# A fused attention and MoE kernel: a new opening list and a new end list, with batch 3's projection further back

## The chip, the cores and the metric

The kernel runs on one core of one Trainium2 chip. Times are device microseconds (us) of one execution; lower is better. The engines are TensorE (PE in the profile; PEld is its weight load), VectorE (DVE), ScalarE (ACT), GpSimd (POOL) and SyncE (SP). Each works through its own instructions in program order and waits on semaphores for the others. Transfers are asked for by POOL (loads from memory that change float32 to bfloat16) or by SP (stores, small reshaping copies, transposes).

## The reference, cut to what matters

```python
def _attn_ref(q, k, v, E, F):                 # q, k, v: 8 batches x 8 heads x 1024 x 64
    k_proj = np.einsum('ks,bhsd->bhkd', E, k)  # the sequence of 1024 projected to 64
    v_proj = np.einsum('ks,bhsd->bhkd', F, v)
    scores = scale * np.matmul(q, k_proj.transpose(0, 1, 3, 2))
    attn = np.exp(scores - np.max(scores, axis=-1, keepdims=True))
    attn = attn / (np.sum(attn, axis=-1, keepdims=True) + 1e-09)
    return np.matmul(attn, v_proj)

def _moe_ref(x, w_in, w_out):                 # x: 8192 x 512, w_in: 512 x 2048, w_out: 2048 x 512
    h = x @ w_in
    g = h * (1.0 / (1.0 + np.exp(-1.702 * h)))
    return g @ w_out
```

The output of the attention, with the heads side by side, is the x of the second function.

## The kernel before, in words

The 8192 tokens are cut into 16 blocks of 512; block j belongs to batch b = j // 2. For a batch, k and v (two loads, line 58, asked for by POOL) are projected with E and F on TensorE (step `pj`, line 671), the projected k is copied (`kb`) and transposed by a DMA of SP (`kd`), the projected v is copied (`vq`). The queries of the batch are loaded in eight pieces (line 70) and transposed by one DMA of SP (`qd`, line 239). For a block there are then scores (`sc`), exponentials on ACT (`ex`), sums (`su`, `den`), the reciprocal of the sums, which takes a way through small DMAs (`ga`, `rc`, `sr`, `sb`), the product with v (`va`), and the division (`mv`). After that come the two large products of the second function. Both are made with seven instead of eight block products (a Strassen form): steps `u0.P1` to `u3.P7` for the first (line 607, four matmuls each), `F1.0` to `F7.1` for the second (line 504, eight matmuls each), with sums of inputs (`xs`, `gs`) and of results (`c1` to `c3`, `d1`, `d2`, `Fc`, `Fd`, `Fo`) on DVE and ACT, and the gelu on ACT (`g11` to `g22`). `st0` and `st1` store half a block of output each.

No scheduler decides an order when the kernel is built. After a prologue, the order is written out by hand in three lists: OPEN, then STEPS, which is repeated for j = 4 to 12, then TAIL. A word such as `pj@6:0` or `kb@6/A` is a step for block 6, with its PSUM bank after the colon and its engine (A for ACT, D for DVE) after the slash. Each step's instructions go to the queues of their engines in the order of the list; there, only the order among steps of one engine and the waits for data remain. A step of SP or POOL that stands late in the list can therefore start early, when nothing holds it.

Two steps ask for loads, and both begin with a tiny copy on POOL into a tile `held`, which makes POOL wait for a chosen event:

```python
        elif i == "ld":
            nc.gpsimd.tensor_copy(held[:, 1], qT[b][:1, J - 1, 0, :1])
            load_kv(k, kt, b + 1, "k_sb")
            load_kv(v, vt, b + 1, "v_sb")
```

So `ld` of batch b waits until that batch's queries are transposed (line 674), and only then asks for k and v of batch b + 1. There is one buffer for k and one for v, so the load also waits for `pj` of batch b. `lq` (line 693) does the same for the queries, waiting for the broadcast `rbc` of the block before. For this case the steps `ld@4` (asks for k and v of batch 3), `pj@6` (projects batch 3), `qd@4` and `qd@6` (transpose the queries of batches 2 and 3) matter most.

Of the kernel before, what the change touches and what calls it, by code (L numbers as in the profile page):

```python
# [17 lines left out]
def kernel(ctx, tc, q, k, v, E, F,  # L18
                                                     moe_w_in, moe_w_out, out):
    nc = tc.nc  # L20
    B, H, S, D = q.shape
# [255 lines left out]
    xs = {}  # L277
# [98 lines left out]
    def ffn2_ops(j):  # L376
# [8 lines left out]
        qda@2 sc.0@1:7,6 sc.1@1:5,4 ex.0.1@1 O.3.0@0:0 ex.1.1@1 ex.1.0@1 ex.0.0@1 O.2.0@0:2 O.1.0@0:1 O.3.1@0  # L385
        tk.2.1@1:6 tk.0.1@1:3 tk.1.1@1:4 tk.0.0@1:5 tk.2.0@1:7 gt@4 O.2.1@0 O.3.2@0 tr.0.0@1 tr.0.1@1 tm.0.1@1
        tm.0.0@1 O.2.2@0 tr.1.1@1 xt.0@1:3 tm.1.1@1 tk.1.0@1:4 O.3.3@0 O.1.1@0 O.2.3@0 tr.2.1@1 tr.1.0@1
        tm.1.0@1 tm.2.1@1 tr.2.0@1 oc.3@0/A tm.2.0@1 O.1.2@0 xt.2@1:6 xt.1@1:0 tk.3.0@1:5 tk.3.1@1:4 xc.2@1/A
        ws.1@1 tr.3.1@1 O.0.0@0:7 O.0.1@0 tr.3.0@1 O.0.2@0 tm.3.1@1 xc.0@1/A tm.3.0@1 xt.3@1:3 O.0.3@0 xc.3@1/A
        xc.1@1/D L.11@1:5 O.1.3@0 L.1@1:4 ws.2@1 ws.0@1 Lg.11@1 oc.2@0/A Lg.1@1 wi.5@1/A oc.0@0/D ws.3@1  # L390
        L.13@1:6 L.3@1:3 L.0@1:7 ws.4@1 pj@2:4 Lg.13@1 vq.0@2/D vx.0@2 Lg.0@1 L.8@1:6 Lg.3@1 kb@2/A oc.1@0/D
        L.14@1:0 L.2@1:2 L.5@1:5 Lg.8@1 kd@2 L.12@1:1 L.4@1:3 Lg.5@1 Lg.14@1 qdb@2 L.6@1:7 L.7@1:0 Lg.12@1
        Lg.4@1 s0.1@0 Lg.6@1 L.10@1:1 L.9@1:3 ws.5@1/D vx.1@2 Lg.7@1 vq.1@2/A Lg.10@1 Lg.2@1 L.15@1:5 Lg.9@1
        Lg.15@1 wi.4@1 sc.1@2:4,6 sc.0@2:7,0 F1.0@1:2 F1.1@1 ex.0.0@2 ex.1.1@2 gs1.0@1 sc.1@3:5,3 ex.1.1@3
        sc.0@3:7,6 Fc1@1:1/D lq@2 gs1.1@1 ex.0.1@3 F2.0@1 ex.1.0@3 ex.0.0@3 s0.0@0 F2.1@1 su@3:7,5 ex.0.1@2
        tk.0.0@2:6 gs3.1@1 gs2.1@1 gs2.0@1 den.0@3/A F6.0@1 den.1@3/D tr.0.0@2 ex.1.0@2 tk.1.0@2:7 tk.1.1@2:0
        tk.0.1@2:3 tm.0.0@2 gs4.1@1 tr.0.1@2 tr.1.0@2 tm.0.1@2 tm.1.0@2 tr.1.1@2 F5.0@1:6 F6.1@1 tk.2.0@2:7
        tk.2.1@2:4 tm.1.1@2 gs3.0@1 F5.1@1 xt.0@2:3 Fc2@1/A xt.1@2:0 tr.2.1@2 tr.2.0@2 ga@3 Fc3@1/A tm.2.0@2
        xc.0@2/A F7.1@1 Fo0@1/A gt@6 tm.2.1@2 xc.1@2/A tk.3.0@2:4 gs4.0@1 xt.2@2:7 tk.3.1@2:3 tr.3.0@2 tr.3.1@2
        rc@3 F3.0@1 xc.2@2/D tm.3.0@2 F3.1@1 F7.0@1 sr@3 u0.P1@2:0 tm.3.1@2 xs.0@2 u1.P5@2:3 u1.P1@2:4 Fd1@1  # L400
        xt.3@2:7 F4.0@1 u0.c1@2:5/D Fd2@1 xc.3@2/A u1.c1@2:2/D u1.c3@2/A xs.1@2 F4.1@1 u0.P2@2 u1.P6@2 xs.3@2
        u1.P3@2 u0.P6@2 u1.P2@2 u2.P1@2:6 Fo1@1/D u1.c2@2/D xs.2@2 u1.P7@2 u0.P5@2:1 u0.c2@2/A u0.g11@2 u1.d2@2
        gt@7 ld@2 u0.P7@2 qd@4 u1.d1@2 u0.c3@2/D u0.d1@2 u1.g11@2 u1.P4@2 u3.P1@2:0 u1.g21@2 u0.P3@2 pj@4:4
        u2.P5@2:2 u1.g22@2 u1.g12@2 u0.d2@2 u0.g12@2 u2.c1@2:3/A kb@4/A u3.c1@2:1/D u2.P6@2 u2.c2@2/D u3.P6@2
        u0.g22@2 u2.P2@2 u3.P5@2:7 u2.c3@2/D vq.1@4/A vq.0@4/D u2.P7@2 u0.P4@2 u3.P2@2 ld@4 u3.c3@2/D u3.c2@2/A
        u3.P7@2 u2.g11@2 u3.g11@2 u3.P3@2 u2.P3@2 u2.d1@2 sb@3 u2.g22@2 u0.g21@2 kd@4 gs1.0@2 u2.P4@2 u3.d1@2
        u2.d2@2 va.0@3:4,5 u2.g21@2 gs2.0@2 u3.P4@2 F1.0@2:3 u3.d2@2 F1.1@2 mv.0.1@3 st0@1 mv.0.0@3 va.1@3:5,7
        u3.g22@2 u2.g12@2 u3.g21@2 u3.g12@2 sc.0@4:4,6 gs1.1@2 Fc1@2:1/A sc.1@4:0,2 F2.0@2 F2.1@2 ex.1.0@4
        ex.1.1@4 ex.0.1@4 xs.0@3 ex.0.0@4 mv.1.1@3 gs2.1@2 F6.0@2 gs4.0@2 Fo0@2/A F6.1@2 st1@1 gs3.0@2
        sc.1@5:6,2 ex.1.1@5 mv.1.0@3 sc.0@5:0,7 su@4:3,4 u0.P1@3:5 xs.1@3 Fc2@2/D den.1@4/A ex.0.1@5 den.0@4/D  # L410
        F5.0@2:2 ex.1.0@5 xs.2@3 u1.P5@3:3 u0.P5@3:7 u0.c1@3:6/D u1.P1@3:4 gs3.1@2 u0.c3@3/D ex.0.0@5 gs4.1@2
        u0.P2@3 u0.g11@3 pj@6:0 xs.3@3 ga@4 u1.c1@3:5/A kb@6/A u0.P3@3 u0.P6@3 u0.c2@3/D u0.d2@3 F7.1@2 F5.1@2
        vq.0@6/A vq.1@6/A u1.P2@3 rc@4 u1.c3@3/A u1.g11@3 su@5:0,7 u0.P7@3 F7.0@2 u0.d1@3 den.1@5/D u1.P6@3
        u1.P3@3 u0.P4@3 u1.c2@3/A u3.P1@3:7 Fc3@2/D den.0@5/A gt@1 lq@4 u0.g12@3 u2.P1@3:4 Fd1@2 F4.0@2
        u3.c1@3:0/D u3.P6@3 u3.P2@3 u1.d2@3 u1.P7@3 kd@6 F4.1@2 u1.g12@3 u2.c1@3:3/D u0.g21@3 u3.g11@3 u0.g22@3
        u1.d1@3 u1.g22@3 sr@4 u2.P6@3 u2.P5@3:6 u3.c2@3/A u1.P4@3 u2.P2@3 u3.P5@3:7 u2.c2@3/A Fo1@2/D u2.g11@3
        u2.c3@3/D u2.P3@3 u2.d2@3 qd@6 u1.g21@3 F3.1@2 sc.1@6:6,4 u3.c3@3/D sc.0@6:5,1 u2.P7@3 F3.0@2 u2.d1@3
        gs1.0@3 ex.1.1@6 u3.P3@3 u2.P4@3 u3.P7@3 sb@4 ga@5 Fd2@2 u3.d1@3 ex.0.1@6 F1.0@3:4 st0@2 gs2.0@3 u3.d2@3
        ex.0.0@6 ex.1.0@6 F1.1@3 u3.P4@3 Fc1@3:1/D va.0@4:6,7 mv.0.1@4 u2.g21@3 va.1@4:5,3 u3.g21@3 F2.1@3
        F2.0@3 mv.0.0@4 st1@2 mv.1.0@4 u2.g22@3 u2.g12@3 u3.g12@3 xs.0@4 u0.P1@4:7 mv.1.1@4 u3.g22@3 u1.P1@4:0  # L420
        u0.c1@4:5/A u1.P5@4:6 gs1.1@3 xs.1@4 Fo0@3/A gs2.1@3 u0.P2@4 gs4.1@3 u1.c1@4:2/A gs3.0@3 xs.3@4 u0.g11@4
        F5.0@3:3 xs.2@4 u1.P2@4 rc@5 u1.c3@4/A gt@5 F6.0@3 F6.1@3 u0.P5@4:7 u1.P6@4 u0.P6@4 u1.P3@4 Fc2@3/D
        F5.1@3 u1.c2@4/D u0.c3@4/A sr@5 u0.c2@4/A u0.P3@4 u1.g11@4 gt@2 u3.P1@4:4 gs3.1@3 u0.P7@4 F7.1@3 F7.0@3
        u0.d2@4 u1.d2@4 u0.d1@4 gs4.0@3 u0.P4@4 Fc3@3/A Fd1@3 gt@3 u1.P7@4 su@6:6,7 F4.0@3 den.1@6/A u3.P5@4:7
        u1.d1@4 u3.c1@4:0/A u3.P2@4 u0.g21@4 den.0@6/A F4.1@3 Fo1@3/D u1.g12@4 u2.P1@4:5 F3.1@3 u3.g11@4
        u2.c1@4:4/D u3.P6@4 u2.P5@4:1 u1.g22@4 u0.g22@4 u2.c3@4/D u3.c3@4/A u0.g12@4 u2.P6@4 u2.P2@4 u3.P3@4
        u3.c2@4/A u2.c2@4/D u2.g11@4 u2.P3@4 u3.P7@4 u3.d2@4 u2.P7@4 u3.d1@4 u1.P4@4 ld@6 F3.0@3 u1.g21@4
        u2.d1@4 u3.g12@4 u2.g22@4 sb@5 Fd2@3 gs1.0@4 u2.P4@4 u3.P4@4 va.0@5:7,5 u2.d2@4 va.1@5:6,2 mv.0.1@5
        st0@3 lq@6 u2.g21@4 u3.g21@4
# [13 lines left out]
        F1.0@13:3 u3.g22@13 ga@15 mv.1.0@14 mv.0.0@14 gs3.0@13 xs.0@14 mv.1.1@14 F1.1@13 u0.P1@14:4 u1.P1@14:0  # L443
        xs.1@14 Fc1@13:1/A u1.c1@14:7/D u2.g12@13 F2.0@13 F2.1@13 Fo0@13/A u0.c1@14:5/A u0.P5@14:6 u1.P5@14:2
        u2.P1@14:3 gs1.1@13 xs.2@14 gs2.1@13 u1.P2@14 gs2.0@13 u0.P2@14 u0.P6@14 u1.P6@14 rc@15 u0.c3@14/D
        u1.g11@14 u1.c3@14/A u0.g11@14 u1.c2@14/D F5.0@13:0 F6.0@13 u0.c2@14/D u1.P7@14 gs3.1@13 u0.P3@14
        F6.1@13 u1.P3@14 u0.P7@14 u0.d2@14 xs.3@14 Fc2@13/A sr@15 u1.d1@14 st1@12 u3.P1@14:6 u3.c1@14:4/A
        u0.g12@14 gs4.0@13 u1.d2@14 gs4.1@13 u2.c1@14:2/A F7.1@13 F7.0@13 F5.1@13 Fc3@13/A u0.d1@14 sb@15
        u2.P2@14 u3.P2@14 u0.P4@14 u2.P6@14 Fd1@13 u1.g12@14 u0.g21@14 u2.g11@14 u1.P4@14 F4.1@13 F4.0@13
        F3.1@13 u3.g11@14 u2.P5@14:5 va.0@15:3,6 u1.g21@14 Fo1@13/A u1.g22@14 u0.g22@14 u2.c2@14/A va.1@15:1,7  # L450
        F3.0@13 mv.0.0@15 mv.1.1@15 mv.0.1@15 Fd2@13 u3.P6@14 u3.P5@14:3 mv.1.0@15 u2.c3@14/A u3.c2@14/A
        u3.c3@14/A u2.P7@14 u2.P3@14 F1.0@14:0 u1.P1@15:6 u3.P3@14 u0.P1@15:7 u3.P7@14 u2.d1@14 xs.0@15 u2.d2@14
        u3.d2@14 xs.1@15 u3.d1@14 F1.1@14 u2.P4@14 u3.P4@14 u0.c1@15:5/A u3.g22@14 u2.g21@14 u2.g12@14 u3.g21@14
        Fc1@14:1/D gs1.0@14 gs3.0@14 xs.3@15 u1.P5@15:3 xs.2@15 u1.c1@15:4/D st0@13 u1.c3@15/D u0.P6@15
        u0.P5@15:2 u0.P2@15 u2.g22@14 u3.g12@14 gs2.0@14 gs1.1@14 u0.c3@15/D st1@13 gs2.1@14 gs3.1@14 F2.0@14
        F2.1@14 u1.P2@15 u1.P3@15 u1.P6@15 Fo0@14/A F5.0@14:0 F5.1@14 F6.1@14 u0.P3@15 u0.g11@15 F6.0@14
        u1.g11@15 u1.c2@15/D u0.c2@15/D Fc3@14/A Fc2@14/A u1.d2@15 u0.d2@15 u3.P1@15:6 u0.g12@15 u2.P1@15:3
        F7.1@14 F7.0@14 gs4.1@14 Fd1@14 u2.c1@15:2/A u2.P2@15 u1.P7@15 u0.P7@15 u2.P6@15 F4.0@14 u2.c2@15/A
        F4.1@14 u0.d1@15 u3.c1@15:7/D u1.d1@15 u2.g11@15 Fo1@14/A u1.g12@15 u3.P2@15 u3.P6@15 u0.P4@15
# [335 lines left out]
```

## Time and profile before

| | us |
|---|---|
| median of 3 runs | 472.89 (472.1 to 473.62) |
| the profiled execution, its own time | 471.61 |
| span of its instructions | 469.8 |
| PE busy in the span | 458.6 (98%) |
| DVE busy | 342.5 (73%) |
| ACT busy | 312.7 (67%) |
| POOL busy | 82.5 (18%) |
| mean granted TensorE clock | 0.996 |

The profiled execution took 1.28 us less than the median, and 1.8 us of it lies around the span. A sum that is made from the profile is therefore made against 471.61 us and then moved to the median. A busy PE in this table includes matmuls that are pipelined, so 98% means that PE seldom lacks work, not that it is at its peak.

### The profile page before, as it was taken

How to read it: one execution, taken by the hardware profiler on the slowest of the kernel's cores; microseconds unless marked ns; L12 is line 12 of the kernel's file. 1: busy time of each engine (PE TensorE's matmuls, PEld its weight loads, DVE VectorE, ACT ScalarE, POOL GpSimd, SP SyncE). 2: the span in 40 equal slices, each digit the busy share in tenths (PEclk: the TensorE clock that was granted, in tenths of full speed). 3: DMA queues.
4: the chain of work that ended last, by engine and by line, in shares of the span. 5: the costliest groups of instructions: out<-in, count | busy, mean ns of one | idle time of the engine just before them, and what ended most of it. 6: DMA issues, size and time to landing. Idle time of an engine off the chain costs nothing.

```text
span 469.8 us, 10622 instructions
## 1 busy us (share of the span) xinstructions
PE 458.6 (98%) x4378; PEld 362.8 (77%) x4378; DVE 342.5 (73%) x617; ACT 312.7 (67%) x541; POOL 82.5 (18%) x111
## 2 busy tenths in 40 slices
PE   8999999996999999999999999999999999999997
PEld 4644547874887888787888878887888888888886
DVE  4545858884687686878778786879679696967772
ACT  2665567585697875958677685858768586656362
POOL 7463116061010601014010410106000000000000
PEclk9999999998999999999999999999999999999999
DMA  9999999999998958979589998899572224152013
GB/s 164 200 188 206 180 190 146 207 238 189 139 235 176 121 136 152 208 156 153 123 138 228 129 152 180 157 186 150 141 142 86 53 93 91 48 137 91 1 64 116
DMA packets 133331, 69.19 MB, mean 147 GB/s; under 512 B 98468, under 2 KB 122532, under 8 KB 133284
## 3 DMA queue, kind: packets, MB, share of 16 engines
q0 software_dynamic: 86496, 29.37, 55.7%
q1 hardware_dynamic: 46708, 38.90, 33.7%
q8 instruction: 34, 0.56, 0.5%
q10 hardware_dynamic: 80, 0.26, 0.2%
q14 instruction: 13, 0.11, 0.1%
HBM read 72.88 MB, written 16.99 MB: 191 GB/s over the span
## 4 chain that ended last, share of the span: by engine, by line
PE 84%; DMA 11%; ACT 2%; POOL 1%; issue 1%; DVE 1%; POOLq 0%; ACTq 0%
PE k_ps L504 36%; PE k_ps L607 33%; DMA v_sb<-in_v_dram 6%; DMA qT<-q_sb 3%; PE k_ps L547 3%; PE k_ps L315 3%; PE k_ps L671 3%; PE k_ps L249 3%; PE k_ps L553 2%; DMA out_dram<-o_sb 1%; POOL k_sb L58 1%; PE k_ps L649 1%; ACT gT L556 1%; POOL v_sb L58 0%; PE k_ps L564 0%
## 5 line engine op out<-in xcount | busy, mean ns | idle before, releaser
L504 PEld LDWEIGHTS <-sg 128*128 128x128 bf16 x960 | 93.6, 98 | 11.3 <-issue 0.4
L607 PEld LDWEIGHTS <-late 128*128 128x128 bf16 x896 | 87.3, 98 | 12.0 <-issue 1.8
L489 DVE TENSOR_TENSOR q_even<-k_ps,q_even 128x512 f32<-128x512 f32 x112 | 74.7, 688 | 23.9 <-PE k_ps L607 22.8
L607 PE MATMUL k_ps<-xw,late 128*128 128x256 bf16 x672 | 89.9, 273 | 0.0
L504 PE MATMUL k_ps<-tw,sg 128*128 128x256 bf16 x720 | 89.2, 273 | 0.0
L504 PEld LDWEIGHTS <-gT 128*128 128x128 bf16 x720 | 68.4, 98 | 17.1 <-issue 9.5
L623 ACT ACTIVATE gT<-k_ps 128x512 bf16<-128x512 f32 x112 | 63.7, 595 | 22.8 <-PE k_ps L607 21.3
L623 ACT ACTIVATE gT<-q_even 128x512 bf16<-128x512 f32 x112 | 65.9, 629 | 15.8 <-DVE q_even L489 15.7
L607 PEld LDWEIGHTS <-w_in_sb 128*128 128x128 bf16 x672 | 65.6, 98 | 9.4 <-issue 1.8
L607 PE MATMUL k_ps<-xT,w_in_sb 128*128 128x256 bf16 x448 | 64.4, 273 | 0.8 <-ACT k_ps L611 0.7
L504 PE MATMUL k_ps<-w_out_sb,gT 128*128 128x256 bf16 x480 | 59.1, 273 | 0.0
L70 POOL DMA_DIRECT2D q_sb<-in_q_dram x56 | 49.0, 905 | 37.7 <-DMA qT<-q_sb 17.9
L374 DVE TENSOR_TENSOR sg<-gT 128x1024 bf16<-128x1024 bf16 x60 | 40.8, 684 | 5.3 <-ACT gT L556 4.2
L643 DVE TENSOR_TENSOR xT<-k_ps,rbc 128x512 bf16<-128x512 f32 x52 | 32.7, 684 | 5.4 <-PE k_ps L249 4.3
L611 ACT COPY k_ps<-k_ps 128x512 f32<-128x512 f32 x37 | 21.2, 574 | 21.0 <-PE k_ps L607 20.0
L607 PE MATMUL k_ps<-xT,late 128*128 128x256 bf16 x224 | 33.3, 273 | 0.0
L635 ACT ACTIVATE expT<-k_ps 128x512 bf16<-128x512 f32 x60 | 32.2, 602 | 0.6 <-PE k_ps L249 0.5
L489 DVE TENSOR_TENSOR o_sb<-k_ps,u_sb 128x512 f32<-128x512 f32 (+1 forms) x31 | 20.8, 670 | 15.8 <-PE k_ps L504 11.9
L607 PE MATMUL k_ps<-xw,w_in_sb 128*128 128x256 bf16 x224 | 31.7, 273 | 0.0
L524 DVE COPY o_sb<-k_ps 128x512 f32<-128x512 f32 x22 | 15.2, 692 | 21.9 <-PE k_ps L504 20.0
L504 PE MATMUL k_ps<-w_out_sb,sg 128*128 128x256 bf16 x240 | 30.8, 273 | 0.0
L504 PE MATMUL k_ps<-tw,gT 128*128 128x256 bf16 x240 | 29.0, 273 | 0.0
(122 smaller groups left out, 542.0 us busy)
## 6 DMA issues: line engine op xcount, KB each, us to landing
out_dram<-o_sb SPq DMA_DIRECT2D x31, 512.0 KB, 5.9
rbc<-rdr SPq DMA_DIRECT2D x26, 512.0 KB, 6.2
k_sb<-in_k_dram POOLq DMA_DIRECT2D x7, 1024.0 KB, 12.3
q_sb<-in_q_dram POOLq DMA_DIRECT2D x56, 128.0 KB, 6.0
v_sb<-in_v_dram POOLq DMA_DIRECT2D x7, 1024.0 KB, 17.4
w_in_sb<-in_moe_w_in_dram POOLq DMA_DIRECT2D x8, 256.0 KB, 11.4
w_out_sb<-in_moe_w_out_dram POOLq DMA_DIRECT2D x4, 512.0 KB, 11.5
v_sb<-in_v_dram POOLq DMA_DIRECT2D x4, 256.0 KB, 10.6
```

The costliest lines, as they stand in the source:

```text
L70: nc.gpsimd.dma_start(out=qt[b][:, j], in_=qv[:, j])
L249: nc.tensor.matmul(outs[i][r.start + c:r.start + c + w], lhsTs[i][ri, c:c + w], rhss[i][ri], start=True, stop=True)
L315: nc.tensor.matmul(h_ps, w_in_sb[:, kc, fc * P:(fc + 1) * P], xT[j][:, kc, ts], start=(kc == 0), stop=(kc == KC - 1))
L374: nc.vector.tensor_tensor(t[i - 1], in0, in1, op=ALU.add if i == 1 else ALU.subtract)
L489: nc.vector.tensor_tensor(out_, in0, in1, op=ALU.add)
L504: nc.tensor.matmul(dst, x[:, k_, t * P:(t + 1) * P], w[:, k_], start=(first and k_ == 0), stop=(final and k_ == FH - 1), skip_group_check= ...
L524: copy(o(int(i[2]))[:, :, :MH], live["FD" if i == "Fo0" else "FB", j])
L607: nc.tensor.matmul(live[h, j][:, r], a[:, k_, f:f + P], w[:, k_], start=(i in (1, 5) and r == 0 and k_ == 0), stop=(i in (2, 3, 4) and r = ...
L611: copy(new(B_, [P, 2, TH]), live[A, j])
L623: nc.scalar.activation(out_, in_, AF.Gelu_apprx_sigmoid)
L635: nc.scalar.activation(expT[j][:, 2 * n + t, :], live[f"S{n}{t}", j], AF.Exp, scale=scale)
L643: nc.vector.tensor_tensor(x_of(j)[:, n, :], live[f"V{p[1]}{t}", j], rbc[j][:, n, :], op=ALU.mult)
```

## The change

The lists OPEN and TAIL are replaced by new ones. STEPS, the prologue and all functions stay. OPEN and TAIL hold the same 1878 steps as before (counted with the repeated STEPS), with the same 4104 matmuls; what differs is their order, PSUM banks, and for 49 copies whether ACT or DVE makes them. In the new opening list `pj@6` stands behind 17 more steps of PE; `pj@4` behind seven more and one fewer; `ld@4` stands further back among its neighbours, and `st1` comes before `st0` for two blocks. The order of POOL's instructions is the same as before. On SP, `qd@6` now comes after `sb@4`, `kd@6` and `ga@5`, where it came before `sb@4` and `ga@5`. In the end list the last two products of PE and the copy `Fo0@15` change places or engines.

The diff, cut to the places that the text speaks of:

```diff
-        qda@2 sc.0@1:7,6 sc.1@1:5,4 ex.0.1@1 O.3.0@0:0 ex.1.1@1 ex.1.0@1 ex.0.0@1 O.2.0@0:2 O.1.0@0:1 O.3.1@0
...
-        gt@7 ld@2 u0.P7@2 qd@4 u1.d1@2 u0.c3@2/D u0.d1@2 u1.g11@2 u1.P4@2 u3.P1@2:0 u1.g21@2 u0.P3@2 pj@4:4
...
-        u0.g22@2 u2.P2@2 u3.P5@2:7 u2.c3@2/D vq.1@4/A vq.0@4/D u2.P7@2 u0.P4@2 u3.P2@2 ld@4 u3.c3@2/D u3.c2@2/A
...
-        u0.P2@3 u0.g11@3 pj@6:0 xs.3@3 ga@4 u1.c1@3:5/A kb@6/A u0.P3@3 u0.P6@3 u0.c2@3/D u0.d2@3 F7.1@2 F5.1@2
...
+        wi.5@1/D sc.1@1:5,6 sc.0@1:7,4 ex.0.0@1 ex.1.1@1 ex.0.1@1 O.2.0@0:3 O.3.0@0:2 O.2.1@0 tk.0.1@1:0 qda@2
...
+        u0.g12@2 pj@4:7 u3.c2@2/A u2.c3@2/A gs1.0@2 u3.P7@2 u2.g11@2 u3.d2@2 u2.c2@2/D gs3.0@2 gs2.0@2 u2.P7@2
...
+        gt@5 u0.d2@3 rc@4 u1.c2@3/A ld@4 u0.P2@3 xs.3@3 u1.P2@3 u0.P7@3 u0.g11@3 F4.1@2 u1.P3@3 u1.P7@3 u0.d1@3
+        u0.P4@3 u2.P1@3:7 F4.0@2 u1.d2@3 su@5:4,3 sr@4 u1.g11@3 pj@6:0 u1.d1@3 sb@4 Fo1@2/D u3.P1@3:2 u1.g12@3
...
-        u0.g21@15 F7.0@15 F7.1@15 fc3.0@15 fc3.1@15 st1@14 u2.g21@15 gs4.0@15 Fd1@15 F2.1@15 F2.0@15 F4.0@15
-        F4.1@15 st0@14 Fo0@15/D gs4.1@15 st0h@15 f3.0@15 f3.1@15 Fo1@15/A st1@15 fd2.0@15 fd2.1@15 st2.0@15
-        st2.1@15
...
+        Fc2@15/A u3.g21@15 u2.g21@15 gs4.0@15 F7.1@15 F7.0@15 fc3.1@15 st0@14 F2.1@15 F2.0@15 Fd1@15 gs4.1@15
+        Fo0@15/A st0h@15 F4.1@15 F4.0@15 f3.1@15 f3.0@15 fd2.0@15 fd2.1@15 Fo1@15/A st1@15 st2.0@15 st2.1@15
```

## The prediction

> **What bounds the kernel now.** I read the table of waits first, since PE is busy for 98% of the span and only a wait of PE can be taken out. For PE, from the first listed step on, it has two rows:
>
> ```profile
> PE k_ps L671 <- DMA v_sb<-in_v_dram: 3.9, 1, 3.9
> PE k_ps L607 <- ACT k_ps L611: 0.7, 1, 0.7
> ```
>
> So a single wait is worth something: a projection (line 671) that waits once for v. The busy time by stretches shows where, and what follows it (columns: PE, PEld, DVE, ACT, POOL, then the granted clock, DMA share, GB/s):
>
> ```profile
> 108.00:110.70 2.70, 2.70 (x26) 2.24 (x23) 2.06 (x5) 2.38 (x5) 0.00 (x0) 1.00 1.24 207
> 110.70:115.00 4.30, 0.42 (x2) 0.11 (x2) 1.49 (x3) 1.89 (x3) 0.88 (x1) 1.00 1.62 189
> 115.00:118.50 3.50, 3.47 (x16) 1.54 (x16) 0.00 (x0) 0.00 (x0) 0.87 (x1) 0.52 2.43 154
> 118.50:122.00 3.50, 3.50 (x38) 2.77 (x38) 1.64 (x3) 2.15 (x5) 0.00 (x0) 1.00 1.47 106
> ```
>
> After the wait the clock is 0.52 for 3.5 us: the whole projection runs at half speed. The chain of waits gives the cause, and the price of an undisturbed projection (last line):
>
> ```profile
> 82.36 14.43 DMA qT<-q_sb
> ...
> 98.95 16.03 DMA v_sb<-in_v_dram
> ...
> 115.03 3.52 PE k_ps L671 x15
> 118.55 0.98 PE k_ps L607 x8
> ...
> 163.96 1.85 PE k_ps L671 x16
> ```
>
> The first line is `qd@4`, the second the load of v for batch 3 that `ld@4` asks for. The projection's first matmul starts at 110.72, the step behind it at 118.5: 7.8 us where 1.85 are needed, so 5.9 us are lost at `pj@6` (3.9 of waiting, 1.6 to 1.7 of half clock, the rest between matmuls).
>
> Then the queues of POOL and SP, for what starts that load:
>
> ```profile
> 96.91 0.17 POOL L674 CAST held<-qT 1x1 f32<-1x1 bf16 x1 [19.09 <-DMA qT<-q_sb]
> 98.08 0.88 POOL L58 DMA_DIRECT2D k_sb<-in_k_dram  x1 [1.01 <-PE k_ps L607]
> 98.95 0.89 POOL L58 DMA_DIRECT2D v_sb<-in_v_dram  x1
> ```
>
> ```profile
> 81.66 0.34 SPq L662 DMA_DIRECT2D rdr<-rc  x1
> 82.36 10.63 SPq L239 DMA_TRANSPOSE qT<-q_sb  x1
> ...
> 119.19 1.19 SPq L681 DMA_TRANSPOSE kt<-k_b  x1
> 121.27 0.33 SPq L662 DMA_DIRECT2D rdr<-rc  x1
> 122.20 5.38 SPq L239 DMA_TRANSPOSE qT<-q_sb  x1
> ```
>
> `sr@3` (81.66) lets SP come to `qd@4`, whose transposes land at 96.8; `held` then frees POOL. The packets of POOL's queue show a gap from 91.7 to 102.9: k is asked for at 98.08 and its first packet moves 4.85 us later. For batch 4 it is 3.8 us (129.72 to 133.56).
>
> **The change part by part.** Every step stays, so the sum of PE's work is the same. What counts is which waits go and which come. A place in a list is told as a time by adding up the PE steps ahead of it from the first listed step (37.1 us on); by 110 the trace runs 2.1 us behind that (`pj@6`: 108.6 by the list, 110.7 in the trace), and I add these 2 us.
>
> 1. *`pj@6` further back.* Seven F steps at 0.873 us (eight matmuls), nine u steps at 0.437 (four) and one `su` at 0.216 now come before it: 6.1 + 3.9 + 0.2 = 10.3 us. In the trace before it starts at 110.7, so it would start at 121.0 without other waits. Is v there? POOL's order is unchanged, and so is SP's up to `qd@4`; only `rc@3`, which `sr@3` waits for, moves. On DVE it now stands behind `tm.3.0`, `tr.3.1`, `tm.3.1` of block 2 (two times 0.35 and 0.13 us), and `tr.3.0` needs a PE step 0.9 us later in the list: 82.2 instead of 81.66, hence about 0.5 us. Then v lands at 115.5; loads of this kind took 15.1 to 18.4 us, so 114.5 to 118. That is 3 us or more ahead of 121.0. `pj@4`, which the load also waits for, ends near 97 (2.6 us later than before), inside POOL's own wait. The loss at `pj@6` goes entirely: −5.9 us.
>
> [...]
>
> What would be late next: `kb@6`, `kd@6`, `qd@6`, and through `held` the loads of batch 4. See the rivals.
>
> 2. *`pj@4` 2.6 us further back.* Its v (asked for at 76.9) was in time before, and the queue ahead of that request is unchanged. `kb@4` moves 3.9 us, `kd@4` on SP likewise, to about 98.5, landing 3.3 us later near 102, before `sc.1@4` (about 105). Cost 0. Without that cover each late microsecond is one of PE. Behind `kd@4` on SP stand the stores of block 1; they go out 3 to 4 us later (about 100.5), and `Fo0@2`, now on DVE at about 107, needs the buffer that one of them frees (5.9 us, so 106.5 to 107.5). 0 to 1 us on DVE; I take 0.
>
> 3. *49 copies between ACT and DVE, new banks, three table loads fewer on ACT* (30 for 33, at 1.28 us). In the opening stretches DVE is busy 13 to 17 of 20 us, ACT 10 to 16. The largest, `wi.5@1` (1.89 us on ACT, 1.22 for this shape on DVE), falls into 3.6 us in which DVE idled from 38.2 on. What new waits the reordering makes the trace can't show. Bound: over the listed part, steps of PE last 11.1 us longer than the median of their kind; 5.9 are `pj@6`, 0.9 is the row of 0.7 above (`u1.c1@4` on ACT stands behind `Fo0@3`, which waits for a store), 0.5 is `sc.0@3`, all others under 0.25 each. A new list can win at most 3 us there, and may lose as much. I take 0, since a gain and a loss have the same bound and nothing decides between them, with ±2 for the range.
>
> 4. *End list.* PE's last step is now `f3.0`, after `f3.1`, but DVE still takes `fd2.0` first. Before, they were spread:
>
> ```profile
> 465.68 0.42 DVE L489 TENSOR_TENSOR o_sb<-k_ps,u_sb 128x256 f32<-128x256 f32 x1 [1.33 <-PE k_ps L504]
> 466.55 0.42 DVE L489 TENSOR_TENSOR o_sb<-k_ps,u_sb 128x256 f32<-128x256 f32 x1 [0.45 <-PE k_ps L504]
> ```
>
> Now both wait for PE's last matmul, and the last store follows two adds and two issues of SP (1.21 us for two) instead of one of each: +0.4 to +0.6, taken as +0.5.
>
> Sum: 471.61 − 5.9 + 0 + 0.5 = 466.2 for an execution like the profiled one. The median stood 1.28 us above it: 467.5.
>
> **The rivals.**
>
> *Small new waits (B).* `pj@6` is served, but `Fo0@2`, `Fo0@3` (its store now stands behind `qd@6` and `sr@5` on SP) or a bank hold PE for 2 to 4 us together. For it: most rows of the opening changed. Against: the old list has only 1.6 us of such waits over 0.25. Time 469.5 to 471.5.
>
> *The slower side: the transposes of `qd@6` come too late (C).* Mechanism: `qd@6` now stands on SP behind `sb@4`, `kd@6` and `ga@5`. `ga@5` waits for `den.0@5`, at 121.6 by the list, so about 123.5; so `qd@6` is issued at about 125 instead of 122.2. Its transposes took 6.9 us there, 14.4 at `qd@4`, where loads of k and v ran beside them, and 10.9 for the next batch. `sc.0@6` reads them; PE reaches it 11.3 us further in the list, at about 137.4. With 125 + 6.9 to 10.9 = 132 to 136 it is served; from a landing after 137.4 on every microsecond is lost. If `qd@6` is issued at 131.6, because a sum on ACT or the rest of SP's row is late, and takes 14.4, it lands at 146: 8.6 us of waiting. [...] It beats the gain from a landing near 142 on. Against it: by 125 the loads of batch 3 are long in, so nothing like the load beside `qd@4` runs.
>
> *The wait moves with the step (D).* If the loads are pushed back as `pj@6` is (the same `held` waits in a later `qd@4`, or batch 4's loads arrive late at `pj@8`), the gain is returned. For batch 4: transposes landing at 134, v asked for at 135.5, in by 150.6 to 154; PE is at `pj@8` near 158 (163.96 less 5.9). 4 us of room, against it. If it happens: 472.9 ± 1.
>
> **How the numbers follow.** The likeliest case (A: `pj@6` served, nothing new above 2 us) gets 0.62, with 465.3 to 469.5 as its own range; B 0.17, C 0.13, D 0.08. About 0.3% (1.4 us) is what a measurement of this kernel can tell from no change. A and B are faster by more than that; D is the same, and a little of B with it: 0.78, 0.09, 0.13. The range of 8 in 10 goes from A's lower end through B: 465.2 to 471.6; it leaves out C and half of D.
>
> **What the new profile would show.** Right: no PE wait for v in the table of waits; the projection of batch 3 near 121, lasting 1.85 us at clock 1.00; `held` near 97.4 and v landing near 115.5; the waits of PE together under 2 us; the two last adds of DVE back to back. Wrong: a scores step (line 249) or line 671 in the table of waits of PE, or a clock below 1.00 between 120 and 165; `qd@6` issued after 128 or landing after 137; v of batch 3 landing after 121.

## The result and the profile after

The changed kernel takes 466.3 us (median of 4 runs, 465.38 to 467.08), the kernel before, measured with it, 472.5 us (471.51 to 473.62): a ratio of 0.9867, 95% interval 0.9837 to 0.9897. A second set of runs gave 0.9875 (0.9851 to 0.9898). The profiled execution took 466.52 us with a span of 464.7; before, these were 471.61 and 469.8. So the profiles differ by 5.1 us and the medians by about 6.2.

PE's waits after the change, from the first listed step on (what PE did, what it waited for: us in total, times, longest):

```profile
PE k_ps L606 <- DVE xT L642: 0.7, 1, 0.7
PE k_ps L606 <- DVE o_sb L523: 0.6, 1, 0.6
PE k_ps L249 <- DVE qT L232: 0.3, 1, 0.3
```

The row for v is gone, and the three that are left make 1.6 us. The busy time by stretches (PE, PEld, DVE, ACT, POOL, then granted clock, DMA share, GB/s):

```profile
110.70:115.00 4.30, 4.30 (x42) 3.86 (x40) 3.93 (x8) 4.05 (x7) 0.88 (x1) 1.00 1.24 206
115.00:118.50 3.50, 3.50 (x35) 3.09 (x33) 2.85 (x6) 1.57 (x3) 0.87 (x1) 1.00 2.23 161
118.50:122.00 3.50, 3.50 (x40) 2.45 (x39) 2.46 (x5) 1.40 (x3) 0.00 (x0) 1.00 2.38 155
122.00:130.00 8.00, 7.95 (x84) 6.10 (x81) 6.17 (x10) 7.90 (x17) 0.00 (x0) 1.00 0.88 153
```

PE is busy throughout and the clock stays at 1.00, while before it stood still for most of the first stretch and ran at 0.52 in the second. The projection of batch 3 now runs from 121.10 to 122.95, that is 1.85 us instead of 7.76. From the first listed step (37.81) to the last (460.01) PE needs 422.2 us; before, it was 428.35. Of these 6.15 us, 5.91 are that one step. That holds for this pair of profiles: in a second profile of the changed kernel (465.3 us span) PE needs 423.5 us and waits 2.4 us in all, so such a sum is good to about 1 us.

POOL's queue shows what it was about. The number in brackets is the idle time ahead of the row, with what ended it:

```profile
97.91 0.17 POOL L673 CAST held<-qT 1x1 f32<-1x1 bf16 x1 [19.19 <-DMA qT<-q_sb]
99.11 0.89 POOL L58 DMA_DIRECT2D k_sb<-in_k_dram  x1 [1.02 <-PE k_ps L606]
99.98 0.88 POOL L58 DMA_DIRECT2D v_sb<-in_v_dram  x1
...
117.09 0.87 POOL L70 DMA_DIRECT2D q_sb<-in_q_dram  x1 [3.98 <-DMA v_sb<-in_v_dram]
...
136.25 0.17 POOL L673 CAST held<-qT 1x1 f32<-1x1 bf16 x1 [18.28 <-DMA qT<-q_sb]
...
156.68 0.88 POOL L70 DMA_DIRECT2D q_sb<-in_q_dram  x1 [2.08 <-DMA v_sb<-in_v_dram]
```

The last row of each load waits for v, so it tells when v landed: about 117.0 for batch 3, 4.1 us ahead of its projection, and about 156.6 for batch 4. The projection of batch 4 starts at 157.75, so there only 1.2 us are left. `held` at 136.25 says when the transposes of `qd@6` had landed; its scores start at 138.69, 2.5 us later. SP's queue, in the same form:

```profile
83.50 10.56 SPq L239 DMA_TRANSPOSE qT<-q_sb  x1
...
117.69 0.33 SPq L661 DMA_DIRECT2D rdr<-rc  x1
123.39 1.28 SPq L665 DMA_DIRECT2D rbc<-rdr  x2
124.72 1.27 SPq L680 DMA_TRANSPOSE kt<-k_b  x1
126.08 0.58 SPq L273 DMA_DIRECT2D rc<-den  x1
126.97 5.75 SPq L239 DMA_TRANSPOSE qT<-q_sb  x1
```

The chain of waits (start, length, what) shows what that order costs on the other side. It now runs through the small copies that carry the reciprocals of block 4:

```profile
111.04 6.25 DMA rc<-den
...
117.69 5.64 DMA rdr<-rc
...
124.06 6.96 DMA rbc<-rdr
...
131.14 1.30 DVE xT L642 x2
...
132.48 0.60 PE k_ps L606 x4
```

`rc` and `rdr` are copies of 16 KB; beside POOL's loads (k and v to 117.0, then the queries to 123.6) each took about 6 us, and PE pays 0.7 us for it at the end (the first row of its waits; 1.2 us in the second profile).

At the end of the kernel both adds of DVE have become one row behind PE's last matmul:

```profile
461.09 0.76 DVE L488 TENSOR_TENSOR o_sb<-k_ps,u_sb 128x256 f32<-128x256 f32 x2 [3.90 <-PE k_ps L503]
```

From PE's last step to the end of the span it is now 4.7 us; it was 4.4.

### The profile page after: what moved, and what is told of

The parts are those of the page before. It is cut to its first block, busy times and chain, and to the rows that moved or that the text cites. A ratio compares the mean times of both kernels' runs of the same rounds, so it can differ in the third digit from the quotient of the medians.

```text
span 464.7 us, 10630 instructions
## 1 busy us (share of the span) xinstructions
PE 455.9 (98%) x4378; PEld 362.1 (78%) x4378; DVE 343.8 (74%) x616; ACT 307.8 (66%) x539; POOL 82.7 (18%) x111
## 4 chain that ended last, share of the span: by engine, by line
PE 85%; DMA 10%; DVE 2%; ACT 1%; issue 1%; POOL 0%; SPq 0%; DVEq 0%; POOLq 0%; ACTq 0%
PE k_ps L503 38%; PE k_ps L606 34%; PE k_ps L249 3%; PE k_ps L552 3%; PE k_ps L546 3%; DMA w_in_sb<-in_moe_w_in_dram 3%; PE k_ps L670 2%; DMA q_even<-in_q_dram 2%; DMA k_sb<-in_k_dram 2%; DMA rbc<-rdr 1%; DMA rc<-den 1%; DMA rdr<-rc 1%; PE k_ps L648 1%; DVE sg L357 0%; PE k_ps L563 0%
## 5 line engine op out<-in xcount | busy, mean ns | idle before, releaser
L610 ACT COPY k_ps<-k_ps 128x512 f32<-128x512 f32 x40 | 23.0, 575 | 23.4 <-PE k_ps L606 22.4
L614 DVE COPY q_even<-k_ps 128x512 f32<-128x512 f32 x37 | 25.2, 684 | 5.2 <-PE k_ps L606 5.1
```

The source lines that it names most:

```text
L610: copy(new(B_, [P, 2, TH]), live[A, j])
L614: copy(u2, live[G, j])
```

## The experiments

All ratios are to the kernel before, which ran on the same chip in the same set. A time as such is compared only within a set.

**Which half of the change: the opening list or the end list.** The new opening list with the old end list:

```diff
 OPEN = new
-TAIL = new
+TAIL = old
```

> The new opening list with the old end list. Theory: the opening carries the whole gain and the new end list costs about 0.4 us, so this is the fastest of the four combinations: 5.5 to 6 us under before, 0.3 to 0.4 under the changed kernel (not to be told from it by the medians; in the profile the last store's add starts 0.35 us earlier behind PE's last matmul). Rival (the end list brings a part): slower than the changed kernel by that part.

Measured: 465.96 against 473.32 us, ratio 0.9853 (0.9833 to 0.9873), some 7 us where 5.5 to 6 were expected. The old opening list with the new end list:

```diff
-OPEN = new
+OPEN = old
 TAIL = new
```

> The old opening list with the new end list. Theory: the wait of 3.9 us for v and the half clock stay; 0.3 to 0.5 us slower than before, which the medians can't show. Rival (the end list brings a part of the gain): faster than before by more than 1 us.

Measured in the same set: 474.31, ratio 1.0019 (1.0000 to 1.0038). The whole gain is in the opening list; the end list, in which 17 of the 49 copies change engine and 20 steps their bank, costs something between nothing and 1.8 us. A third kernel of that set is the changed one with a single swap in the end list:

```diff
-        f3.1@15 f3.0@15
+        f3.0@15 f3.1@15
```

> The changed kernel with f3.0 before f3.1 at the very end, so that DVE's first add no longer waits for PE's last matmul. Theory: the two adds of DVE are spread again, and the end behind the start of PE's last step shrinks from 4.7 to about 4.3 us; 0.35 us less in the span, the rest as in the changed kernel. Rival (the last store's landing sets the end in any case): no change there.

Measured: 466.24, ratio 0.9856 (0.9836 to 0.9876). In the profile the time from PE's last step to the end of the span is 4.34 us, against 4.74 in the changed kernel. So the swap does give back the 0.4 us, but 0.4 us is 0.09% and can't be seen in the ratios.

The kernel with the old opening list had a surprise in its profile. PE's waits:

```profile
PE k_ps L606 <- DVE xw L366: 2.3, 1, 2.3
PE k_ps L670 <- DMA v_sb<-in_v_dram: 2.2, 1, 2.2
PE k_ps L606 <- ACT k_ps L610: 1.1, 1, 1.1
```

The first row does not exist in the profile of before, although the opening list is the same. DVE's timeline shows its source:

```profile
85.73 0.35 DVE L657 RECIPROCAL rc<-rc 128x32 f32<-128x32 f32 x1 [3.49 <-DMA rc<-den]
```

This is `rc@3`. The 16 KB copy `ga@3` that it waits for landed late in this execution, and what stands behind it on DVE kept PE waiting. More on this below.

**The projection alone moved back.** The old lists with `pj@6`, the copies that read it and one sum taken 4.4 us of PE work further back. One copy, `vq.1@6`, also goes from ACT to DVE:

```diff
-        pj@6:0 kb@6/A vq.0@6/A vq.1@6/A su@5:0,7 den.1@5/D   (each at its old place)
...
+        F7.0@2 pj@6:0
...
+        u1.P3@3 su@5:0,7 den.1@5/D
...
+        u0.d1@3 kb@6/A vq.0@6/A vq.1@6/D
```

> The old lists, with pj@6, its copies (kb, vq.0, vq.1), su@5 and den.1@5 alone moved back: 4.4 us of PE work (four u steps, three F steps) now stand between the old and the new place of pj@6. Theory (the late v of batch 3 is all that the change takes away): pj@6 starts near 115.1, v lands near 115.0, the projection lasts 1.85 us at full clock, and about 5 us are gained against before: 467 to 468 us; up to 1 us may be lost at su@5, which needs the bank that pj@6 leaves. Rival (the gain comes from the new order as a whole): less than 2 us gained.

Measured, in the set of the first three kernels: 470.24 against 473.32, ratio 0.9945 (0.9924 to 0.9966). The projection ran at 116.07 for 1.85 us and waited for nothing, and the stretch around it is at full clock, with the DMA share of 2.43 that stood beside the slow projection before:

```profile
115.00:118.50 3.50, 3.50 (x33) 2.13 (x31) 0.90 (x2) 0.91 (x2) 0.87 (x1) 1.00 2.43 155
```

Yet only 3.1 us came of it, between the 5 of the theory and the under 2 of its rival. The waits of PE go some way to say why:

```profile
PE k_ps L606 <- ACT k_ps L610: 1.0, 1, 1.0
PE k_ps L249 <- DVE q_even L614: 0.6, 1, 0.6
PE k_ps L648 <- DVE vq L685: 0.6, 1, 0.6
PE k_ps L606 <- DVE q_even L614: 0.5, 1, 0.5
```

With five more rows of 0.2 to 0.5 they make 4.4 us. The first row is the wait of 0.7 that the kernel before has near 143 (line 611 there), now 1.0; about 3.7 us are new. The rows shown name copies out of PSUM on ACT and DVE (610 and 614 are the copies of the u steps, 685 those of the projection). That the move upset the spacing of these copies is the reading that fits; no run changed the spacing alone.

**What the wait cost in clock.** The old lists with 18 matmuls on zeros put ahead of `pj@6`, so that PE works while it waits; this adds matmuls and removes nothing:

```diff
             kv_ps = new("PJ", [P, H, D])
+            for _ in range(18 if j == 6 else 0):
+                nc.tensor.matmul(kv_ps.rearrange("p h d -> p (h d)"), zeros[:, :P], zeros, start=True, stop=True)
```

> The old lists; ahead of pj@6, 18 matmuls on zeros (128x512, 0.216 us each, 3.9 us together) write the bank that pj@6 then starts anew, so PE works while v is awaited. Theory (1.6 to 1.7 us of the 5.9 lost at pj@6 are the clock, halved by the idle time): pj@6 takes 1.85 us at clock 1.00 after v landed, and about 1.5 us are gained against before: 471. Rival (the slow projection comes from data that arrive late or from the transfers beside it): it still lasts 3.5 us, nothing gained.

Measured: 471.11 against 472.94, ratio 0.9966 (0.9941 to 0.9990), that is 1.8 us by the medians, with an interval of 0.5 to 2.8. The stretch of the projection itself:

```profile
116.40:118.40 2.00, 2.00 (x18) 0.93 (x18) 0.00 (x0) 0.00 (x0) 0.80 (x1) 1.00 2.43 155
```

It takes 1.85 us at clock 1.00 with the same DMA share of 2.43 at which it took 3.5 us at 0.52 before. So the slow projection was the clock after the idle time and not the transfers beside it. Filling this wait was worth 1.8 us of 5.9.

**What held the load up.** The first packet of the load of k moved 4.85 us after its request before the change. The old lists without the two stores of block 1 (that part of the output is not written):

```diff
                 g = int(i[2]) if i != "s0" else t
+                if j == 1:
+                    outs.pop((j, g))
+                    return
```

> The old lists without the two output stores of block 1 (these rows of the output are not written); they stand on SP at 96.7 to 97.7, just ahead of the request for k and v of batch 3 at 98.1. Theory (the load of k and v begins only when what SP has queued before is moved, here transposes, the broadcasts rbc and these stores, until about 104): its first packet comes 3 us earlier, near 99.5 to 100; v lands near 112; pj@6 waits about 1 us and keeps full clock; 4 to 5 us gained against before. Rival (a fixed 4 to 5 us between request and first packet): first packet near 102.9, v near 115, nothing gained.

Measured: 470.33 against 472.94, ratio 0.9938 (0.9916 to 0.9960). The first packet moved 1.8 us after the request (98.17 to 99.98), and the chain of waits has

```profile
99.04 13.99 DMA v_sb<-in_v_dram
113.08 1.89 PE k_ps L674 x15
```

```profile
PE k_ps L674 <- DMA v_sb<-in_v_dram: 1.4, 1, 1.4
PE k_ps L610 <- ACT k_ps L614: 1.1, 1, 1.1
```

The load starts 3 us earlier and v lands 2 us earlier; PE waits 1.4 us for it instead of 3.9, and at 1.4 us the clock stays at 1.00. That gave 2.6 us where 4 to 5 were expected. Of the rest little is explained: the second row is the wait of 0.7 that the kernel before has too (line 611 there), longer by 0.4 us, and 0.6 us of waits for line 646 are new. In this kernel the load's packets stood behind the stores on SP's queue: 4.85 us from request to first packet with them, 1.8 us without.

**The rival: transposes too late.** The changed kernel with `qd@6` moved behind two stores and one small copy on SP, to where its landing passes the scores that need it:

```diff
-        u1.c1@4:6/A qd@6 xs.0@4 F5.1@3
+        u1.c1@4:6/A xs.0@4 F5.1@3
...
+        F6.0@3 st1@2 sr@5 st0@2 qd@6 sc.0@6:7,3
```

> The changed kernel with qd@6 (transposes of the queries of batch 3) moved on SP behind st1@2, sr@5 and st0@2: issued near 136 instead of 127. Theory (the slower-side rival of the prediction, whose price is one microsecond of PE for each that the transposes land after PE comes to sc@6, near 138.7 here): they land near 145, sc.0@6 waits 6 us, at half clock for some 3 us after it; batch 4's loads, asked for behind them, come near 163 where PE, late by 8, is at pj@8 near 166. 6 to 9 us slower than the changed kernel: 472 to 475. Rival (the transposes have room): no change.

Measured: 473.69 against 472.94, ratio 1.0012 (0.9989 to 1.0034). PE's waits and the clock:

```profile
PE k_ps L249 <- DMA qT<-q_sb: 5.2, 1, 5.2
```

```profile
142.00:146.00 4.00, 2.32 (x23) 1.15 (x24) 0.00 (x0) 1.23 (x3) 1.93 (x3) 0.65 0.97 194
146.00:150.00 4.00, 4.00 (x36) 3.47 (x35) 0.68 (x1) 1.37 (x3) 2.60 (x4) 0.92 1.00 176
```

The transposes are issued at 136.29 instead of 126.97 and land near 143.6 instead of 136.2. Against the changed kernel (0.9875) that is 1.4%, or 6.5 us slower. The rival's mechanism and price were right; the changed kernel stays clear of it by 2.5 us.

**The remaining wait of the changed kernel.** First the changed kernel again:

> The changed kernel once more, beside the two below on the same chip: 6 to 7 us under before. In the old opening list rc@3 (DVE) stands ahead of tm.3.0 and tm.3.1 of block 2 and of the copy xc.2, in the new one behind them. Theory (a small copy ga@3 that lands late then holds PE in the old list alone): the profile of this run shows no wait of PE between 82 and 92, whenever ga@3 lands.

Measured: 466.48 against 472.57, ratio 0.9875 (0.9851 to 0.9898). PE has no wait between 82 and 92, but `ga@3` did not land late in this execution, so the theory was not put to the test; two later kernels with the new order, below, speak against it. In the same set, the new opening list and the old end list with one product of the second layer put ahead of the step that waits for `rbc`:

```diff
-        gs2.1@3 mv.1.1@4 u1.P1@4:7 F5.0@3:0 u1.c1@4:6/A qd@6 xs.0@4 F5.1@3 rc@5 F6.1@3 F2.1@3 F2.0@3
+        gs2.1@3 mv.1.1@4 F2.1@3 u1.P1@4:7 F5.0@3:0 u1.c1@4:6/A qd@6 xs.0@4 F5.1@3 rc@5 F6.1@3 F2.0@3
```

> The new opening list with the old end list, and F2.1@3 moved ahead of u1.P1@4, where PE waits 0.7 to 1.3 us for mv@4, which waits for rbc. Theory: PE does F2.1 (0.87 us) in that time and the wait all but goes; 0.7 to 0.9 us under the new opening list with the old end list, 1.0 to 1.3 under the changed kernel, 7 to 8 under before. Rival (the wait moves to the next step that needs mv or a g sum of DVE behind it): no change against the changed kernel but the 0.4 us of the end list.

Measured: 468.42, ratio 0.9910 (0.9885 to 0.9935): 1.7 us slower than the changed kernel by the ratios, 1.9 by the medians, instead of faster. The two intervals just touch; the profile is the firmer evidence. The waits, the clock and ACT's row for the copy:

```profile
PE k_ps L503 <- ACT k_ps L517: 2.4, 1, 2.4
```

```profile
132.00:134.00 2.00, 0.26 (x3) 0.23 (x3) 2.00 (x4) 0.65 (x2) 0.00 (x0) 1.00 1.64 177
134.00:138.00 4.00, 4.00 (x25) 2.94 (x23) 3.03 (x8) 0.57 (x1) 2.04 (x3) 0.60 0.90 316
```

```profile
133.12 0.57 ACT L517 COPY k_ps<-k_ps 128x512 f32<-128x512 f32 x1 [1.04 <-DVE xT L642]
```

The step was no filler. `F2.1@3` adds to what the copy `Fc1@3` (line 517) puts into bank 1, and bank 1 is free only when DVE has read `va.1@4` out of it (line 642), which itself waits for `rbc`. The moved step waited for the very transfer that it should cover, through a PSUM bank; 2.4 us of idle time then cost another 1.6 us at clock 0.60 (4 us at 0.4 below full). These two make more than the 1.7 to 1.9 us measured, in part because the wait of 0.7 to 1.3 us that was to be filled is gone.

**Order or engines.** The changed kernel with the 32 copies of its opening list that had changed engine put back, and its counterpart, the old order with the new engines. "Order" here takes in the PSUM banks (92 steps of the opening change theirs), and the two kernels with the new order have the new end list:

```diff
-        wi.5@1/D oc.3@0/D xc.1@1/A vq.1@2/D xc.2@2/A u1.c3@2/D u0.c2@2/D u1.c2@2/A kb@6/D
+        wi.5@1/A oc.3@0/A xc.1@1/D vq.1@2/A xc.2@2/D u1.c3@2/A u0.c2@2/A u1.c2@2/D kb@6/A
...
```

> The changed kernel with the 32 copies of the opening list that had changed between ACT and DVE put back on the engine they had before; order, banks and end list are the new ones. The projection alone moved back gave 3.1 us, the whole new opening 7.4. If the order makes the difference, this stays at 466 to 468 with PE waits under 3 us together. If the engines of the copies do, the small waits of the kernel with the projection alone moved return (some 4 us of them, behind copies of ACT or DVE at lines 517, 610 and 614) and it takes 469 to 471. The projection of batch 3 starts near 121 and lasts 1.85 us in both cases. I lean to the order, 6 in 10.

> The old order, old banks and old end list, with the 32 copies of the opening list put on the engines that the new list gives them: the fourth cell beside before (old order, old engines), the changed kernel (both new) and new order with old engines (1.0039 of before). If the new engines gain by themselves, some of the 7 us shows here: 468 to 471. If an engine only fits the order that it was chosen for, the wait for v at the projection stays (about 6 us with its half clock) and new waits of 1 to 4 us come behind copies: 473.5 to 477. I expect the second, 8 in 10.

Measured, each against before on its chip:

| | old engines | new engines |
|---|---|---|
| old order | 1 | 1.0078 (1.0057 to 1.0100) |
| new order | 1.0039 (1.0017 to 1.0061) | 0.9875 (0.9851 to 0.9898) |

Each half by itself loses: by the ratios, 3.7 us for the engines and 1.8 us for the order. Together they gain 6. I had leaned to the order, and that was wrong; 474.2 us also lies above both ranges that I gave (466 to 468, 469 to 471). With the old order the forecast of 473.5 to 477 held. In the kernel with the new order and the old engines no wait for v is left, but PE's waits are

```profile
PE k_ps L605 <- DVE xw L366: 1.7, 1, 1.7
PE k_ps L605 <- DVE k_ps L609: 1.4, 2, 1.2
PE k_ps L562 <- ACT expT L633: 1.3, 2, 1.0
PE k_ps L502 <- ACT u_sb L518: 1.1, 1, 1.1
```

With five smaller ones it is 7.5 us. In the kernel with the old order and the new engines the old wait is there, with a clock of 0.51 in the stretch behind it (115.0 to 118.5); beside the rows shown there are five more of 0.2 to 0.7:

```profile
PE k_ps L670 <- DMA v_sb<-in_v_dram: 2.3, 1, 2.3
PE k_ps L249 <- ACT gT L622: 1.6, 1, 1.6
PE k_ps L606 <- ACT k_ps L610: 1.2, 2, 1.0
```

**One of these copies.** `wi.5@1` is the first entry of the list. Put back on ACT alone:

```diff
-        wi.5@1/D sc.1@1:5,6 sc.0@1:7,4
+        wi.5@1/A sc.1@1:5,6 sc.0@1:7,4
```

> The changed kernel with a single copy, wi.5@1, put back from DVE on ACT (1.89 us there). In the kernel with all 32 engines put back, the exponentials that stand behind it on ACT came late and PE waited 1.3 us near 40, with 1.6 us over the usual length of those steps. If waits of PE in the opening are lost for good, this is 1.3 to 1.8 us slower than the changed kernel: 467.6 to 468.3. If a later wait takes it up (the loads of k and v come no later, so the room of the projections grows), 466.3 to 466.8.

Measured: 469.54 against 472.63, ratio 0.9940 (0.9918 to 0.9962). Against the changed kernel's ratio of 0.9875 that is 0.65%, or 3.1 us for a copy of 1.89 us, twice what was expected. ACT's timeline and PE's waits:

```profile
37.25 1.89 ACT L353 CAST late<-sg 128x2048 bf16<-128x2048 f32 x1
39.16 1.28 ACT L633 ACT_TABLE_LOAD   x1
40.45 2.06 ACT L633 ACTIVATE expT<-k_ps 128x512 bf16<-128x512 f32 x4
```

```profile
PE k_ps L605 <- DVE xw L366: 2.2, 1, 2.2
PE k_ps L562 <- ACT expT L633: 1.4, 2, 1.1
```

The second row is the expected one: the table load and the exponentials stand behind the copy. The first was not expected. It is `rc@3` again, which waits 2.54 us for its copy:

```profile
85.44 0.35 DVE L656 RECIPROCAL rc<-rc 128x32 f32<-128x32 f32 x1 [2.54 <-DMA rc<-den]
```

What goes with a late copy can be read off all 14 profiled executions, from the two queues and the packets of `ga@3`:

| opening list up to 76 us | `ga@3` issued, less the request for k of batch 2 (us) | first to last packet of `ga@3` (us) | PE's wait near 84 (us) |
|---|---|---|---|
| new (six executions) | −1.05 to −0.12 | 1.0 to 2.5 | none |
| old (before, projection alone, no stores) | −0.23, −0.18, +0.07 | 1.1 to 1.5 | none |
| old order, new engines | +0.10 | 3.4 | 0.2 |
| old (zero matmuls) | +0.12 | 3.8 | 1.1 |
| old (new end list) | +0.29 | 5.3 | 2.3 |
| new order, old engines | +1.29 | 3.4 | 1.7 |
| `wi.5@1` back | +1.61 | 3.8 | 2.2 |

Issued ahead of the megabyte loads, or up to 0.07 us behind their request, the 16 KB copy got through in 1.0 to 2.5 us; issued 0.1 us or more behind it, its packets were spread over 3.4 to 5.3 us. This is a pattern over 14 profiles; no run moved `ga@3` alone, so it is not shown to be the cause. With `wi.5@1` back, `ga@3` is issued at 77.01 (75.57 to 76.64 in the six) and the request comes at 75.40 (75.95 to 76.95); why the request came earlier stays open. The old list sits on that edge (two of its five executions fell over it), the new list 0.1 to 1.05 us ahead of it. The last two rows answer the theory that came with the repeated run of the changed kernel, that a late `ga@3` holds PE in the old list alone: with the new order PE waited 1.7 and 2.2 us for it too. Only its late landing is rarer there.

## Why the prediction was right, point by point

**Part 1, the projection.** Predicted start 121.0, measured 121.10; 5.9 us taken from the step, measured 5.91. The load was sized a little too early: `held` at 97.91 for 97.4, and the load of v took 17.0 us instead of 16.0, so v landed at 117.0 for 115.5. The room absorbed it. In the 14 profiles every load of v for batch 3 landed at 113 or later, behind the 110.72 at which the projection started before; moved alone to 116.07, it waited for nothing.

What was right in the sum was too simple in the attribution. The prediction let this move bring 5.9 us by itself and everything else nothing. Moved alone it brings 3.1 of the 7.4 us that the opening list brought in that set, and other waits come up (4.4 us, of which 0.7 were there before).

**Part 2, `pj@4`.** Cost 0, as measured: it runs at 94.89 for 1.85 us with no wait.

**Part 3, the copies.** As a net figure 0 ± 2 held: of the 6.15 us only 0.25 lie outside `pj@6`. But the reason given (a gain and a loss with the same bound, nothing to decide between them) hid the largest term of the change. Order and engines taken apart cost 1.8 and 3.7 us, so what the new engines do for the new order is some 8 us. That the net came out near 0 was luck, and not read from anything. The bound of 3 us on either side was taken from what the old list loses; it bounds what can be won, and not what can be lost. Nor does it follow from its figures: 11.1 less 5.9 leaves 5.2 us to win, and the parts named over 0.25 make 1.4 (0.9 and 0.5), not the 1.6 of rival B. The prediction did point to `wi.5@1` as the largest copy and to DVE's idle time that takes it, but put no price on it: it is 3.1 us, much of it through the late `ga@3` (2.2 us of PE's waits).

**Part 4, the end list.** +0.5 predicted, +0.4 in the profile, and the swap of the two products gives it back.

**The sum.** 466.2 was predicted for an execution like the profiled one, and 466.52 came; the prologue took 0.69 us longer in that execution, which was not foreseen and is no part of the change. The median was predicted at 467.5, by carrying over the 1.28 us by which the old median lay above its profile, and came at 466.3. That term failed: the changed kernel's median lies at its profile. A likely reason, argued and not tested, is the late `ga@3`: two of five profiled executions of the old list had it, with 1.1 and 2.3 us of waiting, and none of the six that have the new opening list as it stands up to there.

**The rivals.** B (small new waits, 2 to 4 us together, at 469.5 us or more) did not come: in the four profiles with the new opening and nothing else of bearing, PE's waits make 1.6, 1.7, 1.8 and 2.4 us. One of the signs of being wrong did appear, a row for line 249 among PE's waits; but it is the first listed step at 37.8, which waits 0.3 us for a copy of the prologue, and not `sc.0@6`. C was closer than the prediction had it: `qd@6` was issued at 126.97 instead of 125, since `sb@4` ahead of it on SP waited for a 16 KB copy of 5.64 us, and not, as the prediction had it, since `ga@5` waited for `den.0@5`. It landed at 136.2, at the late end of the 132 to 136 given; 2.5 us were left. D left 1.2 us of room at the projection of batch 4 where 4 were predicted, because the load was asked for 2.1 us later than worked out (137.63 for 135.5) and took 19.0 us.

## What to carry to other kernels

A long wait can be moved away by one step, but in a hand-written order the copies around it have to be placed anew: the new order and the new engines lost 1.8 and 3.7 us alone and gained 6 together, so parts of such a change shouldn't be judged singly. Before a step is put into a gap as filler, follow its PSUM bank and its inputs back: here it waited through a bank for the transfer that it was to cover. Look at the clock behind a long wait of PE before pricing it: here it was 0.50 for 3.41 us behind waits of 2.3 to 5.2 us, which cost up to 1.7 us more, and 1.00 behind two of 2.2 us (next section). Where a chain hangs on a small copy, try to have it issued ahead of large loads: here its packets took 1.0 to 2.5 us from first to last so, and 3.4 to 5.3 us behind them, though no run moved the copy alone.

## What the runs showed of the hardware

**The load of k and SP's requests.** The first packet of POOL's load of k moves 4.85 us (before), 5.6 us (after) and 1.8 us (without two stores) after the request, for batch 4 3.8 us before and 1.7 after. Taking two stores away shortened it by 3 us, so the delay is not a constant of this load. Over the 14 profiles it went by the order of the requests. In eight of them SP issues the two stores of block 1 between 1.7 us before and 0.4 us after the request for k: the delay is 4.85 to 5.6 us. In the other six the stores come 0.9 us or more after it, or not at all: 1.7 to 3.3 us. In the kernel with the zero matmuls they come 0.9 us after it, and from 102 to 107 packets of the load and of the stores move side by side. So in these runs the late first packets go with stores that SP asked for before the load or up to 0.4 us behind it; with stores asked for later the load began sooner, and in one run their packets moved beside the load's. Of the 16.0 us of the load of v before, 4.0 passed ahead of the first packet of k; the two loads then moved in 12.

**Small copies beside large loads.** 16 KB took 5.6 to 6.3 us from issue to landing beside POOL's loads in the changed kernel, and 3.4 to 5.1 us from issue to last packet where `ga@3` got through quickly. In the table above 0.1 to 0.3 us in the order of two requests go with 1.5 or 5.3 us from the copy's first packet to its last.

**The clock.** The traces record each change of the clock. In every one of the 14 all changes lie on a grid of 3.41 us: before the change of the lists they are at 5.73, 114.96, 118.37 and 469.94, that is 32, 1 and 103 times 3.413 us apart; in the changed kernel at 5.66 and 463.05, 134 times 3.413 us apart. In these profiles the falls go with PE's busy share in the 3.41 us that end at a point of the grid. There are five falls within the kernels, after the waits of 3.9, 5.2, 2.3, 2.3 and 2.4 us, and the shares ahead of them are 0.00, 0.00, 0.32 (near 84 with the new end list), 0.31 (`pj@6` with the new engines) and 0.31 (`F2.1@3` as filler). Each lasted 3.41 us at 0.50, which costs up to 1.7 us of work. With the 14 falls at the ends of the kernels, the highest share with a fall behind it is 0.415 (the end of the changed kernel). The lowest without one is 0.424, after the wait of 2.2 us near 84 with `wi.5@1` back; the wait of 2.2 us at `pj@6` with the new end list left 0.49. So in these runs the limit lay near 0.42 (the ends of matmuls are modelled, so the third digit is not safe), which is 2.0 us of idle time in one such stretch: an estimate from these shares. By it a wait of 2.2 us that lies whole in one stretch, with a share of 0.36, would have a fall behind it; the shares of 0.424 and 0.49 say that the grid divided the two that had none.
